# A gated mix of attention and MLP on one core: scores in two 2-bank and three shared 1-bank buffers, a planner that knows the port of VectorE and GpSimd, small scalings on VectorE, two chunks of x transposed by TensorE, another last round

## The chip, the cores and the metric

The kernel runs on one core of one Trainium2 chip. The metric is the device time of one execution in microseconds. Three runs of the kernel before took 892.84, 894.24 and 896.3 us; the median is 894.24 us. Engine names in the rows: PE is TensorE (PEld its weight loads), DVE is VectorE, ACT is ScalarE, POOL is GpSimd, SP is SyncE, which here only issues DMAs.

## The reference

All inputs are bf16; S = 2048 tokens, D = 512, 32 heads of 16, F = 1792.

```python
x = A_x
g = _sigmoid((x * gate_w).sum(-1, keepdims=True))
# A: attention
q, k, v = split_heads(x @ wqkv)                 # 32 heads of 16
p = _softmax(einsum("bhqd,bhkd->bhqk", q, k) * (16 ** -0.5), axis=-1)
a = merge_heads(einsum("bhqk,bhkd->bhqd", p, v)) @ wo
# B: MLP
h = _gelu(_layernorm(x) @ w1)
hs = concat([four 128-column groups of h, shifted by 1, -1, 2, -2 tokens]) @ w2
x1 = x + hs
b = x1 + _gelu(_layernorm(x1) @ w3) @ w4
out = g * a + (1 - g) * b
```

## The kernel before

**Scores.** For each head there are 16 tiles of 128 keys by 512 queries in each of 4 query chunks: 2048 score tiles of 128x512. They are worked off in 32 rounds, one for each chunk c, group G of eight heads and parity p; a round holds 64 tiles, 16 key tiles for each of four heads i that lie in the four 32-row strips of TensorE. A score matmul (L665) writes a tile to PSUM. A tile is exponentiated in one of two ways. ScalarE takes two or three tiles at once from a buffer `psA` of 2 or 3 banks (L741, out `PA`). VectorE takes single tiles from a one-bank `ring` buffer (L766): it turns a score into the bits of a bf16 power of two; two such tiles make a pair of 1024 columns, of which VectorE makes two shifted copies (L790) and GpSimd a third (L793); the four sum to an approximation of exp. A tile of ScalarE thus costs one matmul with V (L821, into `acc`), a tile of VectorE four.

**End of a round.** VectorE copies `acc` to `accsb` (L834, two slots); the row sums go to DRAM and come back 16 to a partition (L837, L839), are inverted and scaled with the gate on VectorE (L841, L842), go out and come back spread over 32 partitions each (L844, L848, `bcs`), GpSimd multiplies (L851, `oT`, two slots), and four DMAs put the result into `oD` (L855, six slots). A slot of `oD` is freed by the output projection of its chunk, which is the tail of the matmul group `w4`.

**Everything else** is a generator ("gen"): groups of column-tiled matmuls (L411) into a ring buffer with one evacuation, mostly on VectorE: the projections of k, q and v, the gate, and w1, w2, w3, w4 of the MLP. The two one-bank ring buffers are shared between gens and VectorE's score tiles. The MLP's layer norms have their statistics and small factors on VectorE and GpSimd, the scaling itself on GpSimd (L529), then go through DRAM and come back by DMA transposes. GpSimd also scales q by two masks (L461), V for the third and fourth copy (L478), and x by 1-g (L587).

**What sets the order.** The order of every engine's instructions is fixed when the kernel is built: a planner (`Sim`) steps through a model of the engines. Each piece of work is a `Job` with an engine, a hold time, dependencies, buffers to take and free, and a priority; `pe_pick` fills TensorE's queue, first scores for free `psA` and ring buffers, then gens and V matmuls until ScalarE is about to be free. A gen may start once as many score tiles have been issued as its `at` says (`spread`, `PLAN`); among the ready ones of the first 24 the one with the smallest `at` goes first. The q of the next group has `at` 128 * r0 - 50, the w4 groups of chunk 0 have 1045 to 1071. On the chip each engine runs its list in order and waits on semaphores.

**Start and end.** Sixteen DMA transposes of x (L364) come first on SP's queue, then x as it stands (L372). The last chunk's output projection (L1053, L1055) follows the last round outside the planner.

## Time and profile before

| what | value |
|---|---|
| median of three runs | 894.24 us |
| the profiled execution | 890.88 us |
| its span, first to last instruction | 888.9 us |
| mean granted TensorE clock | 0.944 |
| ScalarE busy | 755.7 us (85%) |
| TensorE matmul busy (ends modelled) | 786.6 us (89%) |
| VectorE busy | 693.1 us (78%) |
| GpSimd busy | 390.5 us (44%) |

The profiled execution is 3.4 us below the median of the runs, and 2.0 us of it lie outside the span. Busy time of an engine is the union of its instructions; two that follow each other closely overlap by their start-up and drain, so the mean duration of one is longer than what it adds. TensorE's matmuls run four abreast in strips of the array, so its busy share says little about how much more it could take.

### The profile page before, as it was taken

To read this page: it belongs to the slowest core of one execution; us is meant where nothing else is said; L and a number is where in the kernel's file an instruction comes from. 1 tells how busy PE (TensorE), PEld (TensorE's weight loads), DVE (VectorE), ACT (ScalarE), POOL (GpSimd) and SP (SyncE) were. 2 spreads that over 40 slices of the span, in tenths; PEclk is the share of its full clock that TensorE was granted. 3 is DMA by queue.
4 is the path that set the end of the run, shared out by engine and by line. 5 is a ranking of instruction groups with operands and counts; after the bars stand their busy time and mean duration, and the time that the engine had idled before them with its cause. 6 is when DMAs were issued, how large, how long until landed. Compare 5 with 4: busy or idle time off the path is not lost.

```text
span 888.9 us, 22112 instructions
## 1 busy us (share of the span) xinstructions
PE 786.6 (89%) x8981; PEld 251.1 (28%) x8982; DVE 693.1 (78%) x1361; ACT 755.7 (85%) x631; POOL 390.5 (44%) x400
## 2 busy tenths in 40 slices
PE   5996899898898989979898998999988999989982
PEld 1331233322222223322233332333312333323220
DVE  4774988798899998877875787678878568887871
ACT  3364999899998999998993998999998889999990
POOL 2243764444467793434432444234444234344440
PEclk9987999999799999988999996999978999979996
DMA  8512211103013140011000001001000100000001
GB/s 165 168 31 39 82 51 23 38 24 117 17 45 76 46 124 6 18 42 32 14 20 26 24 18 41 26 24 35 18 16 17 30 27 17 14 7 18 18 17 39
DMA packets 71302, 35.83 MB, mean 40 GB/s; under 512 B 51360, under 2 KB 66464, under 8 KB 71200
## 3 DMA queue, kind: packets, MB, share of 16 engines
q1 hardware_dynamic: 68032, 32.84, 14.1%
q10 hardware_dynamic: 3168, 1.57, 0.8%
q8 instruction: 70, 1.15, 0.5%
q14 instruction: 32, 0.26, 0.1%
HBM read 17.60 MB, written 6.82 MB: 27 GB/s over the span
## 4 chain that ended last, share of the span: by engine, by line
PE 48%; ACT 23%; DVE 12%; issue 7%; DMA 4%; POOL 4%; SPq 2%; POOLq 0%; ACTq 0%; DVEq 0%
ACT PA L741 18%; PE acc L821 17%; PE ring L411 17%; PE psA L665 11%; DVE PD L766 5%; DVE PD L790 3%; ACT hT L600 3%; PE ring L665 3%; POOL PD L793 2%; DMA zE_dram<-zE 1%; DVE st L509 1%; POOL xn L529 1%; SPq L364 1%; ACT hT L567 1%; DMA w<-in_A_x_dram 1%
## 5 line engine op out<-in xcount | busy, mean ns | idle before, releaser
L741 ACT ACTIVATE PA<-psA 128x1536 bf16<-128x1536 f32 x614 | 709.7, 1259 | 97.8 <-PE acc L821 38.4
L793 POOL TENSOR_SCALAR PD<-PD 128x1024 uint16<-128x1024 uint16 x257 | 269.8, 1050 | 432.4 <-DVE PD L790 310.4
L766 DVE TENSOR_SCALAR PD<-ring 128x512 uint16<-128x512 f32 x514 | 340.7, 682 | 106.6 <-PE ring L665 90.1
L821 PE MATMUL acc<-PD,V 128*17 128x512 bf16 x2056 | 328.8, 401 | 25.4 <-DVE PD L790 10.5
L821 PE MATMUL acc<-PA,V 128*17 128x512 bf16 x1534 | 292.7, 389 | 2.8 <-DVE accsb L834 2.0
L665 PE MATMUL psA<-q,kT 32*128 32x512 bf16 x1534 | 240.6, 395 | 35.4 <-ACT PA L741 33.5
L790 DVE TENSOR_SCALAR PD<-PD 128x1024 uint16<-128x1024 uint16 x514 | 219.5, 464 | 6.3 <-PE acc L821 0.7
L665 PE MATMUL ring<-q,kT 32*128 32x512 bf16 x514 | 179.1, 402 | 6.1 <-DVE PD L766 5.6
L821 PEld LDWEIGHTS <-V 128*17 128x17 bf16 x3590 | 95.6, 89 | 222.3 <-issue 176.5
L665 PEld LDWEIGHTS <-kT 32*128 32x128 bf16 x2048 | 74.2, 91 | 277.0 <-issue 272.5
L411 PE MATMUL ring<-xnT,w 128*32 128x512 bf16 x1152 | 82.6, 381 | 4.2 <-DVE PD L766 1.3
L411 PE MATMUL ring<-w,hT 128*32 128x512 bf16 x1152 | 84.0, 387 | 1.5 <-DVE x_sb L576 0.8
L411 PEld LDWEIGHTS <-w 128*32 128x32 bf16 x1664 | 45.2, 98 | 56.4 <-issue 32.9
L851 POOL TENSOR_TENSOR oT<-accsb,bcs 128x512 bf16<-128x512 f32 x32 | 41.1, 1283 | 25.1 <-DMA bcs<-rr 18.7
L598 DVE CAST hT<-ring 128x512 bf16<-128x512 f32 x56 | 38.4, 685 | 9.7 <-PE ring L411 9.2
L411 PE MATMUL ring<-w,w 128*32 128x512 bf16 x512 | 44.5, 430 | 1.6 <-DVE PD L766 0.8
L411 PEld LDWEIGHTS <-hT 128*32 128x32 bf16 x1152 | 30.2, 97 | 36.7 <-issue 18.4
L529 POOL TENSOR_SCALAR xn<-x_sb,rs,nm 128x512 bf16<-128x512 bf16 x32 | 29.6, 934 | 1.9 <-DVE nm L522 1.6
L411 PE MATMUL ring<-w,wq 128*32 128x512 bf16 x256 | 20.8, 395 | 8.1 <-DMA w<-in_A_x_dram 6.9
L834 DVE COPY accsb<-acc 128x512 f32<-128x512 f32 x32 | 21.8, 682 | 6.0 <-PE acc L821 5.8
L600 ACT ACTIVATE hT<-hT 128x7168 bf16<-128x7168 bf16 x4 | 24.7, 6177 | 0.0
L509 DVE BATCH_NORM_STATS2 st<-x_sb 128x6 f32<-128x512 bf16 x32 | 21.7, 679 | 0.1
(49 smaller groups left out, 213.4 us busy)
## 6 DMA issues: line engine op xcount, KB each, us to landing
bcs<-rr SPq DMA_DIRECT2D x128, 64.0 KB
xn_dram<-xn SPq DMA_DIRECT2D x32, 128.0 KB
w<-in_B_w_dram SPq DMA_DIRECT2D x5, 512.0 KB
x_sb<-in_A_x_dram SPq DMA_DIRECT2D x4, 512.0 KB
oD<-oT SPq DMA_DIRECT2D x128, 16.0 KB
out_dram<-ot SPq DMA_DIRECT2D x16, 128.0 KB
w<-in_B_w_dram SPq DMA_DIRECT2D x4, 448.0 KB
w<-in_A_wqkv_dram ACTq DMA_DIRECT2D x1, 512.0 KB
```

The source lines that it names most:

```text
L411: units.append([Op("col", j, lambda j=j, lf=lf, rf=rf, st=st, sp=sp: nc.tensor.matmul(get()[32 * j:32 * j + 32, 0:N], lhsT=lf(32 * j, 32 * ...
L509: a = dve(600, deps, lambda: nc.vector.bn_stats(out=sb.slot[:], in_=x_sb[:, t, :]), prio=6, at=at, acq=[sb])
L529: g = gp(760, [m], lambda t=t, xb=xb: nc.gpsimd.tensor_scalar(out=xb.slot[:], in0=x_sb[:, t, :], scalar1=rs[which][:, t:t + 1], scalar2=nm ...
L598: pre.append(evac(g, PSUM_NS, lambda ps, m=m: nc.vector.tensor_copy(out=h2[:, m, :], in_=ps[:]), acq=[bb] if m == 0 else []))
L600: ge = act(93 + 427 * FT + 2600, pre, lambda: nc.scalar.activation(out=h2, in_=h2, func=ACT.Gelu_apprx_tanh), prio=0)
L665: o = Op("row", i, lambda: nc.tensor.matmul(dst(), lhsT=kT[G][32 * i:32 * i + 32, kt * P:(kt + 1) * P], rhs=qbuf[G, c].slot[32 * i:32 * i ...
L741: job = act(hold, ops, lambda: nc.scalar.activation(out=pb.slot[:, 0:n], in_=buf.slot[:, 0:n], func=ACT.Exp, scale=0.25), acq=[pb], frees= ...
L766: nc.vector.tensor_scalar(out=pr["buf"].slot[:, h * 512:(h + 1) * 512], in0=buf.slot[:], scalar1=BITS_MUL, scalar2=BITS_ADD, op0=ALU.mult, ...
L790: nc.vector.tensor_scalar(out=d[k][:, 0:w], in0=d[0][:, 0:w], scalar1=float(SHIFT * k), scalar2=None, op0=ALU.add)
L793: nc.gpsimd.tensor_scalar(out=d[k][:, 0:w], in0=d[2][:, 0:w], scalar1=1.0, scalar2=float(SHIFT), op0=ALU.mult, op1=ALU.add)
L821: o = Op("col", i, lambda: nc.tensor.matmul(acc[32 * i:32 * i + DH + 1, :], lhsT=lhs(), rhs=rhs(), start=st, stop=True, tile_position=(0, ...
L851: n = gp(1250, d3, lambda: nc.gpsimd.tensor_tensor(out=ob.slot[:], in0=ab.slot[:], in1=bb.slot[:], op=ALU.mult), acq=[ob], frees=[ab, bb], ...
```

## The change

- ScalarE's score buffers are two of two banks (before three and two); the ring has three one-bank buffers (before two); `PA` has nine slots (before six).
- The planner marks jobs with `port`: all of GpSimd's, and VectorE's fast SBUF-to-SBUF ones. A marked job isn't started while another holds the port. VectorE's priorities are finer; a pair also takes a token that its GpSimd copy gives back; rounds are kept within 10 to 12 tiles of each other; a DMA holds SP's queue for 450 or 1280 ns in the model (before 60).
- Gens have a due time; the ready one that is due first goes first, and one that is overdue goes ahead of the V matmuls. The q of the next group may start 110 tiles ahead and is due 150 ahead of its first tile.
- The masks of q, the layer norms' scaling, the scaled V and (1-g) x are computed on VectorE.
- Chunks 0 and 1 of x come in as they stand and are transposed by TensorE (32 matmuls of 128x128 against an identity), chunks 2 and 3 by DMA as before. V is projected in two halves of 16 heads, the second between tiles 110 and 253. The exp table is loaded by a dummy activation.
- The last round's row sums are brought to all partitions by matmuls with an identity, the MLP's result of the last chunk is put into PSUM by such a matmul, and the last group's four heads go through their own weight `woL`; no DMA lies between the last score and the output.

In numbers of instructions: exps on ScalarE from 307 of three tiles and 306 of two (and one of one) to 716 of two (and one of one); tiles of VectorE (L766, now L891) 514 to 615; shifted copies on VectorE (L790, now L920) 514 to 614 of 1024 columns and two of 512; copies on GpSimd (L793, now L923) 257 to 307 and one of 512; matmuls 8,982 to 9,679.

```diff
-    WIDTHS, RING = (3, 2), 2
-    NPA, NPD, NW = 6, 16, 9
+    WIDTHS, RING = (2, 2), 3
+    NPA, NPD, NW = 9, 16, 9
...
-            if any(not self.free[b.cls] for b in j.acq):
+            if any(not self.free[b.cls] for b in j.acq) or j.port and self.lock > self.t:
...
+        if j.port:
+            self.lock = self.t + j.hold
...
+    xa, xb = (start(e, 2100.0, lambda q, a=a: q.dma_start(out=x_sb[:, a:a + 2, :], in_=x_src(0, a, a + 2)))
+              for e, a in (("SP", 0), ("ACT", 2)))
...
+    def x_transposes(c, half, dep):
+        g = gen("t", -1, dep + [j_id], [], due=-9 + half)
+        ks = (2 * half, 2 * half + 1)
+        g.units = [[Op("full", None, lambda k=k, t=t: nc.tensor.transpose(
+            out=g.buf.slot[:].bitcast(BF16)[:, (k % 2) * 512 + t * P:(k % 2) * 512 + (t + 1) * P],
+            in_=x_sb[:, 4 * c + t, k * P:(k + 1) * P], identity=idb[:]), ns=54.0, name="t") for t in range(4)]
+            for k in ks]
...
-            j_q[G, c, p] = gp(680, [e, j_m3] + ([j_q[G, c, 0]] if p else []), lambda p=p, m=m: nc.gpsimd.tensor_scalar(
-                out=qb.slot[:, p, :], in0=qf.slot[:], scalar1=m[:], scalar2=1.0, op0=ALU.mult, op1=ALU.mult), prio=0,
+            j_q[G, c, p] = dve(205, [e, j_m3] + ([j_q[G, c, 0]] if p else []), lambda p=p, m=m: nc.vector.tensor_scalar(
+                out=qb.slot[:, p, :], in0=qf.slot[:], scalar1=m[:], scalar2=None, op0=ALU.mult), prio=0.3, port=True,
...
-            g = gp(760, [m], lambda t=t, xb=xb: nc.gpsimd.tensor_scalar(
+            g = dve(205, [m], lambda t=t, xb=xb: nc.vector.tensor_scalar(
...
-            q_proj(G, c, 128 * r0 - 50)
+            q_proj(G, c, 128 * r0 - QAT)
...
-        for g in gens[:24]:
-            if g.at > sim.tiles:
-                break
-            if not sim.free["ring"]:
-                return None
-            if all(d.done is not None for d in g.deps):
-                return g
-        return None
+        if not sim.free["ring"]:
+            return None
+        best = None
+        for g in gens:
+            if g.at <= sim.tiles and (best is None or g.due < best.due) and all(d.done is not None for d in g.deps):
+                best = g
+        return best
...
+        if g is not None and g.due <= sim.tiles:
+            do_gen()
...
+    nc.scalar.copy(out=ab[:, 256:512], in_=acc[:, 256:512])
+    nc.vector.tensor_copy(out=ab[:, 0:256], in_=acc[:, 0:256])
+    for b in range(4):
+        nc.tensor.matmul(pd[:, 4 * b:4 * b + 4], lhsT=ab[:, b * P:(b + 1) * P], rhs=idf[:, 0:P:32], start=True, stop=True)
...
+    nc.vector.reciprocal(out=rdl[:], in_=pd.rearrange("p (b j) -> p b j", j=4))
...
+            nc.tensor.matmul(bc[32 * j:32 * j + 32, b * P:(b + 1) * P], lhsT=rdl[:, b, j:j + 1].to_broadcast([P, 32]),
+                             rhs=idf[:], start=True, stop=True, tile_position=(0, 32 * j), skip_group_check=True)
```

SP's queue at the start of the program, before; `w` are chunks of transposed x, `x_sb` is x as it stands:

```order
L364 DMA_TRANSPOSE w_121<-in_A_x_dram 128x512 x4
L364 DMA_TRANSPOSE w_122<-in_A_x_dram 128x512 x4
L364 DMA_TRANSPOSE w_123<-in_A_x_dram 128x512 x4
L364 DMA_TRANSPOSE w_124<-in_A_x_dram 128x512 x4
L372 DMA x_sb<-in_A_x_dram 128x4x512 x4
```

The same queue now:

```order
L414 DMA x_sb<-in_A_x_dram 128x2x512
L419 DMA x_sb<-in_A_x_dram 128x4x512
L412 DMA w_135<-in_A_wqkv_dram 128x4x256
L423 DMA_TRANSPOSE w_132<-in_A_x_dram 128x512 x4
L412 DMA w_134<-in_A_wqkv_dram 128x4x384
L412 DMA wq<-in_A_wqkv_dram 128x4x384
L423 DMA_TRANSPOSE w_133<-in_A_x_dram 128x512 x4
L412 DMA w_135<-in_A_wqkv_dram 128x4x256
```

The plain loads of x stand first, and eight of the sixteen transposes are left.

VectorE where chunk 0's output rows (`ot`) are made, before; the `accsb` copy here ends round 16, and `qf` is the q of chunk 2's second group:

```order
L766 TENSOR_SCALAR PD_107<-ring_97 128x512
L624 SCALAR_TENSOR_TENSOR ot_152<-ring_98,omg,x_sb 128x512
L766 TENSOR_SCALAR PD_107<-ring_97 128x512
L790 TENSOR_SCALAR PD_115<-PD_107 128x1024
L790 TENSOR_SCALAR PD_111<-PD_107 128x1024
L624 SCALAR_TENSOR_TENSOR ot_153<-ring_98,omg,x_sb 128x512
L598 CAST hT<-ring_98 128x512 x2
L459 CAST qf_138<-ring_98 128x512
L834 COPY accsb_140<-acc 128x512
L598 CAST hT<-ring_98 128x512
L766 TENSOR_SCALAR PD_113<-ring_97 128x512
```

The same place now; the `accsb` copy here ends round 15, one round earlier, and the two q masks stand on VectorE:

```order
L891 TENSOR_SCALAR PD_129<-ring_100 128x512
L748 SCALAR_TENSOR_TENSOR ot_161<-ring_102,omg,x_sb 128x512
L920 TENSOR_SCALAR PD_124<-PD_129 128x1024
L920 TENSOR_SCALAR PD_114<-PD_129 128x1024
L748 SCALAR_TENSOR_TENSOR ot_162<-ring_101,omg,x_sb 128x512
L748 SCALAR_TENSOR_TENSOR ot_161<-ring_100,omg,x_sb 128x512
L970 COPY accsb_150<-acc 128x512
L891 TENSOR_SCALAR PD_119<-ring_102 128x512
L562 CAST qf_147<-ring_100 128x512
L920 TENSOR_SCALAR PD_117<-PD_119 128x1024
L564 TENSOR_SCALAR q_146<-qf_147,mE 128x512
```

Chunk 0's output rows come a round earlier against the ends of the rounds, and six evacuations in a row (`ot`, `hT`, `hT`, `qf`, `accsb`, `hT`) have become three.

VectorE at the end of the program, before:

```order
L790 TENSOR_SCALAR PD_117<-PD_108 128x1024
L834 COPY accsb_141<-acc 128x512
L841 RECIPROCAL pk_159<-pk_159 128x16
L842 TENSOR_TENSOR pk_159<-pk_159,gpk 128x16
L1055 SCALAR_TENSOR_TENSOR ot_152<-ring_97,omg,x_sb 128x512
```

The same end now:

```order
L920 TENSOR_SCALAR PD_121<-PD_120 128x512
L1201 COPY accsb_150<-acc 128x256
L1208 RECIPROCAL rdl<-psA_103 128x16
L1209 TENSOR_TENSOR rdl<-rdl,zE 128x16
L1215 TENSOR_TENSOR oT_154<-accsb_150,psA_103 128x256 x2
L1226 TENSOR_SCALAR ot_161<-ring_100,omg 128x512
```

Before, a DMA stands between `accsb` and the reciprocal and again between the scaled `pk` and the last rows; now each row's input is in PSUM or SBUF.

## Rows read from the trace of the kernel before

**Rows 1.** The page: span, and each engine's busy time, share and instructions.

```profile
span 888.9 us, 22112 instructions
PE 786.6 (89%) x8981; PEld 251.1 (28%) x8982; DVE 693.1 (78%) x1361; ACT 755.7 (85%) x631; POOL 390.5 (44%) x400
```

**Rows 2.** Windows: stretch, length, busy us by engine (instructions), clock, DMA share, GB/s.

```profile
0.00:100.00 100.00, 79.14 (x858) 25.68 (x858) 64.26 (x133) 53.14 (x47) 38.80 (x52) 0.91 0.41 97
100.00:850.00 750.00, 687.85 (x7990) 219.78 (x7989) 613.40 (x1199) 688.10 (x573) 342.93 (x341) 0.96 0.12 33
850.00:889.00 39.00, 19.66 (x140) 5.67 (x135) 15.40 (x31) 14.45 (x14) 8.77 (x8) 0.77 0.11 32
200.00:300.00 100.00, 90.23 (x970) 27.14 (x967) 90.39 (x183) 93.76 (x76) 61.17 (x66) 0.95 0.23 64
...
126.40:156.10 29.70, 28.53 (x333) 9.38 (x331) 25.63 (x52) 29.62 (x26) 12.65 (x14) 1.00 0.15 34
```

**Rows 3.** Lines by form: shapes, count, busy us, mean ns, idle before, releasers.

```profile
L741 ACT ACTIVATE PA<-psA 128x1536 bf16<-128x1536 f32 x307 | 451.8, 1472 | 81.8 <-PE ring L665 31.5 <-PE acc L821 30.1 <-PE psA L665 18.8
L766 DVE TENSOR_SCALAR PD<-ring 128x512 uint16<-128x512 f32 x514 | 340.7, 682 | 106.6 <-PE ring L665 90.1 <-PE psA L665 15.2
...
L741 ACT ACTIVATE PA<-psA 128x1024 bf16<-128x1024 f32 x306 | 320.5, 1047 | 15.9 <-PE acc L821 8.3 <-PE psA L665 5.9 <-PE ring L665 1.4
...
L793 POOL TENSOR_SCALAR PD<-PD 128x1024 uint16<-128x1024 uint16 x257 | 269.8, 1050 | 432.4 <-DVE PD L790 310.4 <-PE ring L665 40.1 <-PE acc L821 34.3
...
L790 DVE TENSOR_SCALAR PD<-PD 128x1024 uint16<-128x1024 uint16 x514 | 219.5, 464 | 6.3 <-PE acc L821 0.7
...
L529 POOL TENSOR_SCALAR xn<-x_sb,rs,nm 128x512 bf16<-128x512 bf16 x32 | 29.6, 934 | 1.9 <-DVE nm L522 1.6
```

**Rows 4.** Timeline of ScalarE, 10 to 100 us: start, length, what, idle before it.

```profile
12.56 2.37 ACT L741 ACTIVATE PA<-psA 128x1536 bf16<-128x1536 f32 x2
...
27.89 2.37 ACT L741 ACTIVATE PA<-psA 128x1536 bf16<-128x1536 f32 x2 [5.88 <-PE acc L821]
...
82.67 2.53 ACT L741 ACTIVATE PA<-psA 128x1536 bf16<-128x1536 f32 x2 [9.52 <-PE psA L665]
```

**Rows 5.** Timeline of VectorE, 64 to 84 us.

```profile
77.86 0.25 DVE L841 RECIPROCAL pk<-pk 128x16 f32<-128x16 f32 x1 [7.95 <-DMA pk<-den]
```

**Rows 6.** Timeline of SP's queue, 0 to 64 us.

```profile
0.72 20.79 SPq L364 DMA_TRANSPOSE w<-in_A_x_dram  x16
```

**Rows 7.** Timeline of all engines, 472 to 492 us.

```profile
480.87 1.04 PE L411 MATMUL ring<-wo,oD 128*32 128x512 bf16 x16
...
483.12 5.07 SPq L855 DMA_DIRECT2D oD<-oT  x8
...
486.38 1.27 POOL L851 TENSOR_TENSOR oT<-accsb,bcs 128x512 bf16<-128x512 f32 x1 [6.43 <-DMA oD<-oT]
...
489.70 3.73 ACT L741 ACTIVATE PA<-psA 128x1536 bf16<-128x1536 f32 x3 [14.58 <-PE acc L821]
```

**Rows 8.** The chain that ended last, from 845 us: start, length, what.

```profile
863.04 1.45 ACT PA L741
...
866.16 1.69 DMA den<-accsb
...
879.84 5.55 PE ring L1053 x13
885.41 0.75 DVE ot L1055
```

**Rows 9.** Timeline of VectorE, 128 to 140 us: two shifts, then two tiles.

```profile
131.83 0.76 DVE L790 TENSOR_SCALAR PD<-PD 128x1024 uint16<-128x1024 uint16 x2
132.51 1.28 DVE L766 TENSOR_SCALAR PD<-ring 128x512 uint16<-128x512 f32 x2
```

**Rows 10.** Timeline of GpSimd and VectorE, 857 to 863 us.

```profile
858.46 1.27 POOL L851 TENSOR_TENSOR oT<-accsb,bcs 128x512 bf16<-128x512 f32 x1
...
858.80 1.55 DVE L790 TENSOR_SCALAR PD<-PD 128x1024 uint16<-128x1024 uint16 x2
```

364 lines of the change are left out of this document (249 added, 115 removed).

## The prediction

> **What bounds the kernel now.** I read the page's busy shares first, then the windows, because the shares average over three different stages, then the lines by form, and at last the timelines of the two ends and of the longest wait of ScalarE. On the page [rows 1] ScalarE is busy 85% of the span, TensorE 89% with modelled ends, VectorE 78%, GpSimd 44%: no engine is full. The windows [rows 2] show why. In the first 100 us ScalarE works 53.14 us, so 46.9 us are lost; from 100 to 850 us it works 688.1 of 750, 61.9 lost; of the last 39 us it works 14.45, 24.5 lost. In the middle ScalarE sets the pace: in a stretch that nothing disturbs (126.4 to 156.1 us) it is busy 29.62 of 29.70 us while VectorE is busy 25.63. So a change pays by what it takes from ScalarE in the middle, as long as another engine does not fill up first, and by what it takes from the two ends.
>
> The ends. ScalarE's first exp starts at 12.56 us, and it waits again and again for V matmuls, since score buffers and PA are full while V is not there: 5.88 us before 27.89, 9.52 us before 82.67 [rows 4]. SP's queue is busy with 16 transposes of x for 20.79 us [rows 6]. At the other end the last exp ends at 863.04 + 1.45 = 864.5 us, and 24.4 us pass to the end of the span: the first DMA hop starts at 866.16 and the last matmuls only at 879.84 [rows 8], so 13.7 us of DMA hops, one small multiplication and waits lie between.
>
> The longest wait: before 489.70 us ScalarE stands for 14.58 us [rows 7]. The rows tell the chain. The output projection of chunk 0 (L411 from oD) runs until 481.9; only then are oD slots free, SP issues eight oD DMAs from 483.12 on, GpSimd's oT, which had waited 6.43 us for them, runs at 486.38, an accsb slot comes free, and the round can end. No score of a later round was allowed to run meanwhile.
>
> **The change part by part.** The sum is made against the profiled execution, 890.9 us, and moved to the runs' median at the end.
>
> *The last round.* What goes: 13.7 us between the first hop and the last matmuls, of which GpSimd's multiplication is 1.3. What stays: V matmuls, a copy of acc (two halves on two engines), output, its DMA; 885.41 + 0.75 = 886.2 to 888.9 is 2.7 us for that DMA. What is new on the path: four small matmuls, a reciprocal and a small product, 20 matmuls that start the fourth bank, 16 that spread the factors, two half-width products, 16 output matmuls, two evacuations one after the other on each of two engines. For matmuls I take the pace of the old last ones with their waits, 13 in 5.55 us, as upper bound of a group of four (0.43 us) [rows 8]: about 14 groups, at most 6 us, and 3 if they run close; full fp32 operands have no row here and may double that. The VectorE steps are 0.68 us at most, as L766 [rows 3], half for half the width: about 3.4 us. So 0.5 + 3.4 + 4 + 2.7 = 10.6 us after the last exp instead of 24.4. I take -13 us, with -10 (matmuls twice as dear) and -15.5 as ends.
>
> *The start.* Eight transposes of 1.30 us (20.79 / 16) leave SP's queue and half of V's projection leaves the first rounds; the first chunk is transposed from a plain load, so the first exp should start at about 10 to 11 us. The waits on V matmuls shrink with V, and nine PA slots stand in place of six. What stays, at least in part, is the 9.52 us wait: VectorE stood for 7.95 us before the reciprocal of round 0's row sums, whose DMA came behind the gate's way through DRAM [rows 5], and the product behind it needs the gate in both programs. Of the 46.9 us I take a third: -16, with -6 (only the earlier exp and half of the queue) and -25 as ends.
>
> *The long wait.* Chunk 0's output rows stand a round earlier against the rounds in VectorE's new list, and the block of six evacuations is three. I take -12 of 14.6, with -4 and -14.6 as ends. If oD slots still come late, the wait is back.
>
> *The middle, ScalarE's side.* A column costs (1472 - 1047) / 512 = 0.83 ns [rows 3]. 1433 tiles in place of 1534 are 51,712 columns less: -42.9 us. But there are 103 instructions more, and each has a fixed part: 1047 - 850 = 197 ns alone, less the overlap of neighbours, which is 0.12 us (a mean of 1.26 against 29.62 / 26 = 1.14 in the undisturbed stretch [rows 2, 3]): 0.077 x 103 = +7.9. Together -35, of which 573 / 614 fall in the middle: -33.
>
> *The middle, VectorE's side.* 101 tiles more at 0.60 us (1.28 us for two, less one drain [rows 9]) are 61 us; 101 shifts more at 0.34 (131.83 to 132.51 holds two) are 34 us. 90 scalings come over from GpSimd: 32 xn, 30 q, 16 V, 12 x. No row shows one on VectorE; a shift of twice their columns takes 0.34, so they lie between 0.17 (half) and 0.34; I take 0.21 as some part is fixed: 19 us, 15 to 31. GpSimd loses these (32 xn alone were 29.6 us at 934 ns) and gains 50 copies of 1.05: 52 us. It stays far from full. VectorE goes from 693 to 807 us if nothing else changes. Two things can give some back. The shifts took 219.5 / 514 = 0.427 us each against 0.38 in an undisturbed pair: 24 us are collisions with GpSimd, and the new list puts two tiles between a pair's shifts and the next shifts, beside which GpSimd's 1.05 us fits. And L766 counts 0.66 us each (340.7 / 514) since many stand alone; close behind each other they take 0.60: 31 us. So 752 to 807 us.
>
> In the middle, VectorE's 613.4 us become 668 to 719, in 735 us of old time (750 less the wait). The best 100 us that I find hold 90.39 [rows 2]. At that share VectorE would need 739 to 795 us, that is +4 to +60; by ScalarE alone the middle would take 735 - 33. I take -8: VectorE at its lower figure and 92% busy, a little above the best seen, because the added work (shifts, tiles) has its input ready earlier with a third ring buffer and the list was made with the port in it. TensorE gets 8% more matmuls (9,679 for 8,982) and two refills for each pair of exps where a smaller buffer drains in 0.93 us in place of 1.35; that is a reason not to take more.
>
> A row on the port: VectorE's two shifts at 858.80 took 1.55 us instead of 0.76; GpSimd's oT ran from 858.46 to 859.73 [rows 10]. The first shift started and got nowhere until GpSimd was done: 0.79 us lost. The Trainium skill, "SBUF — State Buffer", section "Who interferes with whom", says that VectorE in its two-port modes and GpSimd exclude each other for the whole instruction, whichever comes first. The trace agrees with it in this row, and by that rule each of the 90 scalings moved to VectorE adds a place where this can happen.
>
> Sum: 890.9 - 13 - 16 - 12 - 8 = 842, and 845 against the median, which lies 3.4 above the profiled execution.
>
> **The rivals.**
>
> *ScalarE keeps its whole gain.* VectorE and TensorE have room, idle gaps stay as they are: 845 - 25 = 820. For it: 18% of VectorE's middle is idle today. Against: the same gaps must now take over 50 us of work.
>
> *VectorE is the bound.* It stays near 90% with collisions avoided only in part: +4 to +30 in the middle in place of -8, 857 to 883, some 868. For it: nothing busier than 90.39 is seen. Against: in that window gens and layer norms crowd it, too.
>
> *Slower.* The place is the port in the middle: real times slip against the planner's, and the 706 fast VectorE operations meet GpSimd's 354 or so long ones by chance. The price is 0.79 us for each meeting [rows 10]; today it is 24 us, some 30 such meetings. On a full VectorE each lies on the path. From about 68 more than forecast, (899 - 845) / 0.79, the kernel is slower than before: one operation in seven, some 900 us. Against: today it is one in seventeen without any planning.
>
> *It doesn't do what it says.* The long wait stays, since oD still has six slots: 857; this falls into the second rival's stretch.
>
> **How the numbers follow.** The forecast, 832 to 857 us: 0.49. ScalarE alone, 810 to 832: 0.19. VectorE as bound, 857 to 885: 0.25. Port, 899 and more: 0.05. Rest 0.02. The range for 8 in 10 is 818 to 876: it takes in most of the first rival and two thirds of the second. Half a per cent is about what a measurement of this kernel can tell from no change (890 to 899 us): faster 0.93, same 0.03, slower 0.04.
>
> **What the new profile would show.** The last exp's end to the end of the span: about 11 us in place of 24.4. ScalarE's idle time in the first 100 us: about 31 in place of 46.9, with the first exp at 10 to 11. No wait of ScalarE over 5 us between 100 us and the end. L920 at 0.39 or so a piece by busy time in place of 0.427; above 0.5 the port rival holds. The 512-column scalings about 0.2 us in place. VectorE's middle at 92% busy or above; if ScalarE is over 95% busy there, the first rival holds. I am wrong if the middle takes longer for each round than now, or if ScalarE idles over 45 us in the first 100.

## The result and the profile after

The changed kernel takes 860.8 us (median of four runs, 859.9 to 861.8); the kernel before, run beside it, took 893.54. The ratio is 0.9633 (95% interval 0.9602 to 0.9663). The time lies inside the range of 818 to 876 us, but 16 us above the forecast of 845 and just outside its own band of 832 to 857. The profiled execution took 860.45 us, its span 858.7 at a mean granted TensorE clock of 0.962 (before 0.944); how much of the gain is the clock's, no run separates.

The page of the changed kernel, where [rows 1] stood for before:

```profile
span 858.7 us, 24104 instructions
PE 794.5 (93%) x9715; PEld 253.8 (30%) x9715; DVE 785.6 (91%) x1657; ACT 735.1 (86%) x743; POOL 379.6 (44%) x369
```

VectorE has 92 us more work in a span that is 30 us shorter. ScalarE has only 20.6 us less. The windows of the changed kernel (start:end, length, then busy us of TensorE, its weight loads, VectorE, ScalarE and GpSimd with instructions, clock, DMA share, GB/s), the counterpart of [rows 2]:

```profile
0.00:100.00 100.00, 89.00 (x1302) 35.83 (x1302) 83.31 (x196) 74.84 (x82) 35.59 (x45) 0.93 0.40 94
100.00:820.00 720.00, 674.53 (x8077) 206.06 (x8074) 678.34 (x1414) 638.81 (x638) 331.66 (x313) 0.97 0.13 34
820.00:859.00 39.00, 31.01 (x342) 11.96 (x339) 23.91 (x50) 21.44 (x25) 12.39 (x12) 0.94 0.09 24
```

In the middle TensorE is 93.7% busy, VectorE 94.2% and ScalarE 88.7%. Before, ScalarE and TensorE stood there at 91.7% each (688.10 and 687.85 of 750 us) [rows 2]; the prediction named ScalarE alone as what sets the pace. VectorE went past the 90.39% that I had found as its best, and still did not carry ScalarE along.

The same in ScalarE's time, by the two profiled executions (us):

| part | before | after | difference | forecast |
|---|---|---|---|---|
| ScalarE's work | 755.7 | 735.1 | -20.6 | -33 |
| its idle time in the first 100 us | 46.9 | 25.2 | -21.7 | -16 |
| its idle time after the last exp | 23.9 | 14.6 | -9.3 | -13 |
| the longest wait of the middle | 14.6 | 8.7 | -5.9 | -12 |
| its other idle time in the middle | 47.8 | 75.1 | +27.3 | +25 |
| span | 888.9 | 858.7 | -30.2 | -49 |

Before, a last exp of one tile ends at 864.98 us, after the one at 864.49 that the prediction took for the last, so 23.9 us follow it and not 24.4. Now 16.3 follow, of which ScalarE works 1.75. In the column of forecasts the middle's -8 is split into ScalarE's side, -33, and the +25 of idle time that remains. Of the 19 us by which the sum was missed, 12 are ScalarE's own work, 6 the long wait, 4 the last round and 2 the idle time of the middle; the start gave 6 more than forecast.

The ends of the rounds tell the same more plainly. Each is a copy of `acc` (L834 before, L970 and for the last one L1200 now); here are the times at which some of them start (us):

| round | before | after | lead of the changed kernel |
|---|---|---|---|
| 0 | 62.7 | 41.4 | 21.3 |
| 14 | 424.1 | 410.7 | 13.4 |
| 15 | 446.6 | 441.9 | 4.7 |
| 16 | 488.2 | 465.6 | 22.6 |
| 31 | 865.4 | 844.0 | 21.4 |
| end of the span | 888.9 | 858.7 | 30.2 |

The whole lead at the last round was there at the end of the first. Up to round 15 the changed kernel loses some 16 us of it, the long wait of the kernel before gives that back in round 16, and the 15 rounds after that take as long as before. So the middle, long wait and all, gave nothing, where -20 was forecast; the gain is 21 us at the start and 9 after the last round.

The lines of the changed kernel by form (line, engine, out<-in, shapes, count | busy us, mean ns | idle before and what ended it), the counterpart of [rows 3]:

```profile
L866 ACT ACTIVATE PA<-psA 128x1024 bf16<-128x1024 f32 x716 | 683.9, 1029 | 100.5 <-PE ring L789 51.6 <-PE psA L789 38.7 <-remote 5.6
L891 DVE TENSOR_SCALAR PD<-ring 128x512 uint16<-128x512 f32 x615 | 400.9, 679 | 26.9 <-PE ring L789 18.9 <-remote 5.6 <-POOL PD L923 0.7
...
L920 DVE TENSOR_SCALAR PD<-PD 128x1024 uint16<-128x1024 uint16 x614 | 260.1, 464 | 1.8
...
L636 DVE TENSOR_SCALAR xn<-x_sb,rs,nm 128x512 bf16<-128x512 bf16 x32 | 11.3, 405 | 0.0
...
L564 DVE TENSOR_SCALAR q<-qf,mE 128x512 bf16<-128x512 bf16 x15 | 5.4, 357 | 0.0
...
L694 DVE TENSOR_SCALAR x_sb<-x_sb,omg 128x512 bf16<-128x512 bf16 x12 | 4.2, 414 | 0.0
...
L978 DVE TENSOR_TENSOR pk<-pk,gpk 128x16 f32<-128x16 f32 x31 | 5.0, 162 | 2.9 <-DMA gpk<-zE_dram 2.9
...
L629 DVE SCALAR_TENSOR_TENSOR nm<-mv,rs 128x4 f32<-128x4 f32 x8 | 1.1, 142 | 0.0
```

Of ScalarE's 100.5 us of idle time before exps 90.3 are put down to score matmuls (L789), in 119 waits of which the longest is 8.7 us. I read them as the refill of two-bank buffers and, for the ones put down to `ring`, the matmul ahead of it in TensorE's queue. The shifts stayed at 0.424 us each (260.1 / 614; 0.427 before). In the traces 38 of the 614 last over 0.55 us, 40 of 514 before; all 38 start while an operation of GpSimd runs, and what they take beyond the median of 0.42 us comes to 28.9 us (23.6 before). So these collisions were not planned away. The 512-column scalings that came over cost 0.35 to 0.41 us, not 0.21.

ScalarE's timeline in the first 100 us, the counterpart of [rows 4]:

```profile
11.32 0.59 ACT L536 CAST kT<-ring 128x512 bf16<-128x512 f32 x1 [2.57 <-PE ring L495]
12.53 4.70 ACT L866 ACTIVATE PA<-psA 128x1024 bf16<-128x1024 f32 x5 [0.62 <-PE psA L789]
...
63.62 4.97 ACT L866 ACTIVATE PA<-psA 128x1024 bf16<-128x1024 f32 x5 [5.59 <-remote]
```

The first exp is no earlier than before (12.53 for 12.56). The gain of this stretch is that ScalarE waits less on V afterwards: before, 22.1 us in the first 100 were put down to V matmuls (`acc`), now none. A wait of 5.59 us ends at 63.62, put down to "remote", that is, to no event that the profile has. VectorE stands at the same time:

```profile
63.59 0.69 DVE L891 TENSOR_SCALAR PD<-ring 128x512 uint16<-128x512 f32 x1 [5.55 <-remote]
```

SP's queue in these microseconds; L606 writes the gate's 2048 numbers to DRAM, L609 reads them back and waits for that:

```profile
52.13 0.39 SPq L606 DMA_DIRECT2D zE_dram<-zE  x1
53.49 1.15 SPq L646 DMA_TRANSPOSE xnT<-xn_dram  x1
63.68 2.70 SPq L609 DMA_DIRECT2D gpk<-zE_dram  x4
```

The two engines go on within 0.1 us of the issue at 63.68, for which the gate's DMA, which left at 52.13, has to have landed. TensorE stood too, and ran at half its clock afterwards. Its timeline, and the window of 63.6 to 71 us (columns as in the windows above):

```profile
64.69 0.61 PE L789 MATMUL psA<-q,kT 32*128 32x512 bf16 x2 [4.79 <-ACT PA L866]
```

```profile
63.60:71.00 7.40, 5.19 (x52) 1.84 (x51) 4.55 (x10) 4.90 (x5) 1.05 (x1) 0.50 0.28 57
```

The same DMA took 11.3 us in the kernel before (issued at 66.39, read at 77.66), and TensorE stood for 7.0 us there, up to 78.45; the prediction's 9.52 us wait of ScalarE is at this place.

All engines where chunk 0's output rows (`ot`) are made, the counterpart of [rows 7]:

```profile
437.32 0.75 DVE L748 SCALAR_TENSOR_TENSOR ot<-ring,omg,x_sb 128x512 bf16<-128x512 f32 x1 [3.92 <-PE ring L495]
...
441.20 0.75 DVE L748 SCALAR_TENSOR_TENSOR ot<-ring,omg,x_sb 128x512 bf16<-128x512 f32 x1 [3.13 <-PE ring L495]
...
441.87 0.68 DVE L970 COPY accsb<-acc 128x512 f32<-128x512 f32 x1
...
442.02 1.94 ACT L866 ACTIVATE PA<-psA 128x1024 bf16<-128x1024 f32 x2 [8.72 <-PE psA L789]
```

VectorE stands twice for output-projection matmuls, the `accsb` copy that ends round 15 is queued behind, and ScalarE waits 8.72 us. The cause is not the old one: GpSimd's `oT` no longer waits for oD slots (L987 waits for `bcs` alone). TensorE's part is this window:

```profile
432.13:441.53 9.40, 9.40 (x156) 4.27 (x155) 2.35 (x5) 1.17 (x2) 1.62 (x2) 1.00 0.09 30
```

TensorE is busy throughout, by its modelled ends: 144 matmuls of two `w4` groups with their output projection stand in its list in a row, nine V matmuls among them and no score.

All engines at the end of the changed kernel, the counterpart of [rows 8]:

```profile
837.17 5.20 ACT L866 ACTIVATE PA<-psA 128x1024 bf16<-128x1024 f32 x6
...
844.45 0.42 DVE L1201 COPY accsb<-acc 128x256 f32<-128x256 f32 x1 [3.10 <-ACT accsb L1200]
...
847.71 1.42 PE L495 MATMUL ring<-wo,oD 128*32 128x512 bf16 x12
...
849.07 1.05 PE L1203 MATMUL psA<-idf,accsb 128*128 128x4 f32 x8
...
854.07 0.69 ACT L1224 ACTIVATE ot<-ring,omg 128x512 bf16<-128x512 f32 x1 [9.65 <-PE ring L1221]
```

The last exp ends at 842.37, and 16.3 us follow instead of 10.6. The copies of `acc` start at 844.04, 1.2 us later than forecast, and are done at 844.87, but the matmuls that read them (L1203) start at 849.07, behind output-projection matmuls (L495) that were let into TensorE's queue only after the last score.

### The profile page after: what moved, and what is told of

It reads as the page before. It is cut to its first block, busy times and chain, and to the rows that moved or that the text cites. A ratio compares the mean times of both kernels' runs of the same rounds, so it can differ in the third digit from the quotient of the medians.

```text
span 858.7 us, 24104 instructions
## 1 busy us (share of the span) xinstructions
PE 794.5 (93%) x9715; PEld 253.8 (30%) x9715; DVE 785.6 (91%) x1657; ACT 735.1 (86%) x743; POOL 379.6 (44%) x369
## 4 chain that ended last, share of the span: by engine, by line
PE 41%; DVE 36%; ACT 11%; issue 5%; DMA 5%; SPq 1%; ACTq 0%; POOL 0%; DVEq 0%; POOLq 0%
PE acc L954 15%; PE ring L495 14%; DVE PD L891 14%; DVE PD L920 11%; PE psA L789 11%; ACT PA L866 7%; ACT hT L707 2%; DMA pk<-den 2%; DVE st L616 2%; DMA zE_dram<-zE 1%; DVE accsb L970 1%; DVE hT L706 1%; DVE x_sb L685 1%; DVE V L579 1%; DVE xn L636 1%
## 5 line engine op out<-in xcount | busy, mean ns | idle before, releaser
L866 ACT ACTIVATE PA<-psA 128x1024 bf16<-128x1024 f32 x717 | 684.4, 1029 | 100.5 <-PE ring L789 51.6
L923 POOL TENSOR_SCALAR PD<-PD 128x1024 uint16<-128x1024 uint16 x308 | 326.1, 1060 | 446.4 <-DVE PD L920 298.1
L891 DVE TENSOR_SCALAR PD<-ring 128x512 uint16<-128x512 f32 x615 | 400.9, 679 | 26.9 <-PE ring L789 18.9
L954 PE MATMUL acc<-PD,V 128*17 128x512 bf16 x2460 | 339.5, 395 | 21.1 <-DVE PD L920 7.4
L789 PE MATMUL psA<-q,kT 32*128 32x512 bf16 x1433 | 270.7, 392 | 23.8 <-ACT PA L866 22.4
L954 PE MATMUL acc<-PA,V 128*17 128x512 bf16 x1433 | 283.4, 388 | 0.4 <-DVE accsb L970 0.4
L920 DVE TENSOR_SCALAR PD<-PD 128x1024 uint16<-128x1024 uint16 x616 | 260.5, 464 | 1.8
L789 PE MATMUL ring<-q,kT 32*128 32x512 bf16 x615 | 201.7, 398 | 5.9 <-DVE PD L891 5.5
L789 PEld LDWEIGHTS <-kT 32*128 32x128 bf16 x2048 | 72.6, 91 | 286.0 <-issue 284.0
L495 PE MATMUL ring<-xnT,w 128*32 128x512 bf16 x1152 | 84.8, 382 | 1.6 <-DVE PD L891 1.3
L495 PE MATMUL ring<-w,hT 128*32 128x512 bf16 x1152 | 81.3, 388 | 1.1 <-DVE PD L891 0.9
L495 PEld LDWEIGHTS <-w 128*32 128x32 bf16 x1920 | 45.3, 96 | 49.6 <-issue 32.9
L987 POOL TENSOR_TENSOR oT<-accsb,bcs 128x512 bf16<-128x512 f32 x31 | 40.6, 1311 | 9.4 <-DMA bcs<-rr 9.4
L495 PEld LDWEIGHTS <-hT 128*32 128x32 bf16 x1152 | 28.3, 97 | 37.7 <-issue 19.2
L495 PE MATMUL ring<-w,w 128*32 128x256 bf16 (+1 forms) x768 | 36.2, 316 | 0.7 <-DVE PD L891 0.4
L970 DVE COPY accsb<-acc 128x512 f32<-128x512 f32 x31 | 21.1, 679 | 2.7 <-PE acc L954 2.7
L495 PE MATMUL ring<-wo,oD 128*32 128x512 bf16 x240 | 20.9, 380 | 0.0
L495 PE MATMUL ring<-w,wq 128*32 128x512 bf16 x256 | 18.4, 382 | 2.3 <-DVE PD L891 1.4
```

Of the source, the lines that this page charges most:

```text
L495: units.append([Op("col", j, lambda j=j, lf=lf, rf=rf, n0=n0, n1=n1, st=st, sp=sp: nc.tensor.matmul(get()[32 * j:32 * j + 32, n0:n1], lhsT ...
L789: o = Op("row", i, lambda: nc.tensor.matmul(dst(), lhsT=kT[G][32 * i:32 * i + 32, kt * P:(kt + 1) * P], rhs=qbuf[G, c].slot[32 * i:32 * i ...
L866: job = act(hold, ops, lambda: nc.scalar.activation(out=pb.slot[:, 0:n], in_=buf.slot[:, 0:n], func=ACT.Exp, scale=0.25), acq=[pb], frees= ...
L891: nc.vector.tensor_scalar(out=pr["buf"].slot[:, h * 512:(h + 1) * 512], in0=buf.slot[:], scalar1=BITS_MUL, scalar2=BITS_ADD, op0=ALU.mult, ...
L920: nc.vector.tensor_scalar(out=d[k][:, 0:w], in0=d[0][:, 0:w], scalar1=float(SHIFT * k), scalar2=None, op0=ALU.add)
L923: nc.gpsimd.tensor_scalar(out=d[k][:, 0:w], in0=d[0 if both else 2][:, 0:w], scalar1=1.0, scalar2=float(SHIFT * (k if both else 1)), op0=A ...
```

## The experiments

Each was run beside the kernel before on the same chip; the ratio is to that. The changed kernel's own ratio is 0.9633 (0.9602 to 0.9663), 860.8 us. A ratio's interval reaches 3 to 5 us to either side, so differences of a few us are not settled. All but the first two were planned anew, so each has another order of everything.

**Is VectorE the bound? Less of its shifts.** From pair 20 on:

```diff
+                    w_ = w if k == 1 or num < 20 else 256
-                    nc.vector.tensor_scalar(out=d[k][:, 0:w], in0=d[0][:, 0:w], ...
+                    nc.vector.tensor_scalar(out=d[k][:, 0:w_], in0=d[0][:, 0:w_], ...
```

> The changed kernel with the same order, in which from the 21st pair on VectorE's second shifted copy covers 256 of its 1024 columns only; the rest of that buffer keeps older bits, so part of the attention is not computed. VectorE loses some 287 x 0.20 = 57 us of work, no other engine loses any. Theory (VectorE is what bounds the middle): 30 to 50 us faster than the changed kernel, 811 to 831 us. Rival 1 (TensorE's list is the bound): within 8 us of 861. Rival 2 (no engine, the waits between them in a balanced order): 10 to 25 us faster, 836 to 851.

845.5 us, ratio 0.9467 (0.9426 to 0.9508). The shifts in the lines by form of this run:

```profile
L922 DVE TENSOR_SCALAR PD<-PD 128x1024 uint16<-128x1024 uint16 x327 | 140.2, 433 | 1.8
L922 DVE TENSOR_SCALAR PD<-PD 128x256 uint16<-128x256 uint16 x288 | 89.6, 311 | 0.0
```

A shift of a quarter of the columns still takes 0.311 us by this view, so the groups lost 30.3 us (260.1 less 229.8); VectorE's busy time on the page fell by 46.8 (785.6 to 738.8), which I put down to the end of a short shift lying beside the next instruction. The kernel gained 15, as rival 2 had it: a half to a third of what was taken away. VectorE bounds it only in part.

**Is TensorE the bound? Fewer V matmuls.** The fourth copy's matmuls with V are left out from pair 20 on:

```diff
+                leave = k == 3 and num >= 20
...
-        o = Op("col", i, lambda: nc.tensor.matmul(acc[...], lhsT=lhs(), rhs=rhs(), ...
+        o = Op("col", i, None if leave else lambda: nc.tensor.matmul(acc[...], lhsT=lhs(), rhs=rhs(), ...
```

> The changed kernel with the same order, in which from the 21st pair on the V matmuls of the fourth copy (GpSimd's) are left out, so part of the attention is not computed. TensorE loses 574 matmuls, 574 / 4 x 0.22 = 31 us of its list, and no longer waits for GpSimd there; VectorE and ScalarE lose nothing. Theory (VectorE bounds the middle): within 8 us of 861. Rival 1 (TensorE bounds it): 20 to 31 us faster, 830 to 841. Rival 2 (waits in a balanced order): 8 to 18 us faster.

853.56 us, 0.9558 (0.9522 to 0.9594): 7 us, just inside the theory's 8 and by its interval not apart from rival 2; rival 1 with its 20 us fell. But the 31 us are an estimate that this run does not bear out: by the page TensorE's busy time fell by 11.5 us only (794.5 to 783.0). 7 us for 11.5 is a larger part than VectorE's, so TensorE as what bounds the middle is not excluded. The two results together say that work comes back in part at either engine.

**The scalings back on GpSimd.** The four small scalings as before, the rest of the change kept:

```diff
-            g = dve(205, [m], lambda t=t, xb=xb: nc.vector.tensor_scalar(
+            g = gp(760, [m], lambda t=t, xb=xb: nc.gpsimd.tensor_scalar(
```

and the same for q, V and (1-g) x.

> The changed kernel with the 90 small scalings (layer norms' output, q masks, scaled V, (1-g) x) on GpSimd again, planned anew with the port in the model. VectorE loses about 30 us by the new trace (90 merged scalings), GpSimd gains some 65. Theory (VectorE bounds the middle): 8 to 25 us faster, 836 to 853. Rival (the port: GpSimd's long scalings hold up VectorE's shifts, and q comes later): 3 to 15 us slower, 864 to 876, with the busy time of a shift above 0.45 us.

876.8 us, 0.9809 (0.9775 to 0.9844). From the lines by form of this run:

```profile
L920 DVE TENSOR_SCALAR PD<-PD 128x1024 uint16<-128x1024 uint16 x626 | 279.3, 493 | 2.1
```

The rival came, a little beyond its range, with the shift just short of its 0.45. GpSimd's busy time rises to 448.3 us and a shift to 0.446 us (279.3 / 626): 65 shifts last over 0.55 us where 38 did, and what they take beyond the median goes from 28.9 to 45.9 us. So VectorE, with 30 us of scalings taken away, is 6.5 us busier (792.1); 12 more tiles and shifts of the new plan are in that, too. Moving the scalings was worth 16 us, although VectorE pays 0.35 to 0.41 us for each. How much of the 16 is the shifts' and how much comes of q being later was not separated.

**The planner without the port.** The lock is never set, so GpSimd's and VectorE's marked jobs may be planned together:

```diff
-            self.lock = self.t + j.hold
+            self.lock = 0.0
```

> The changed kernel planned without the port: VectorE's fast jobs and GpSimd's are placed as if they never met; all else as it is. Theory (the port in the model keeps VectorE's shifts out of GpSimd's way and VectorE is full): 8 to 25 us slower than the changed kernel, 869 to 886, with the busy time of a shift 0.45 us or more in place of 0.423. Rival (the two tiles between the shifts do it anyway): within 6 us of 861, and the shift as it is.

874.95 us, 0.9793 (0.9744 to 0.9841), as the theory had it in time. But the shifts stay at 0.427 us. The collisions show elsewhere; from the lines by form of this run:

```profile
L978 DVE TENSOR_TENSOR pk<-pk,gpk 128x16 f32<-128x16 f32 x31 | 9.0, 290 | 4.4 <-DMA gpk<-zE_dram 4.3
...
L564 DVE TENSOR_SCALAR q<-qf,mE 128x512 bf16<-128x512 bf16 x15 | 6.7, 447 | 0.0
...
L629 DVE SCALAR_TENSOR_TENSOR nm<-mv,rs 128x4 f32<-128x4 f32 x8 | 5.2, 656 | 0.0
```

The same `nm` of four columns took 142 ns in the changed kernel and takes 656 here, `pk` 162 and 290. The two stood between in the kernel before:

```profile
L842 DVE TENSOR_TENSOR pk<-pk,gpk 128x16 f32<-128x16 f32 x32 | 8.4, 262 | 1.8 <-DMA gpk<-zE_dram 1.5
...
L522 DVE SCALAR_TENSOR_TENSOR nm<-mv,rs 128x4 f32<-128x4 f32 x8 | 3.6, 453 | 0.6 <-POOL rs L520 0.6
```

VectorE is busy 797.6 us, 12 more. The port's cost, 0.79 us in one meeting [rows 10], is real, and the planner avoids it for these small operations; that the shifts would show it was wrong (42 of 618 last over 0.55 us here, 38 of 614 with the lock). That the 12 us are what makes the 14 is likely and not shown, since the order is another one. The Trainium skill, "SBUF — State Buffer", section "Who interferes with whom", which lets a two-port operation of VectorE and GpSimd exclude each other for a whole instruction, agrees with the q rows. The same section says that an operation of VectorE with two SBUF inputs contends with GpSimd's reads; `nm` and `pk`, which have two, bear that out with 0.51 and 0.13 us on average.

**The buffers alone undone.** The whole change but with score buffers of three and two banks, two ring buffers and six PA slots (the last round's fourth and third bank placed to fit):

```diff
-    WIDTHS, RING = (2, 2), 3
-    NPA, NPD, NW = 9, 16, 9
+    WIDTHS, RING = (3, 2), 2
+    NPA, NPD, NW = 6, 16, 9
```

> The changed kernel planned with ScalarE's score buffers of three and two banks, two shared one-bank buffers and six PA slots of 1536 columns, as before the change; the third and fourth bank of the last output come from ScalarE's buffers. ScalarE then has about 51,000 columns more by way of more of its tiles (0.83 ns each, +40 us of work), VectorE some 120 tiles less. Theory (the new buffers move work from ScalarE to VectorE and ease both ways of waiting): 8 to 25 us slower than the changed kernel, 869 to 886. Rival (balanced already, buffers don't matter): within 6 us of 861.

851.97 us, 0.9549 (0.9507 to 0.9591): 9 us faster than with the new buffers, intervals just apart. The theory fell. The page of this run:

```profile
span 850.2 us, 22779 instructions
PE 780.5 (92%) x9337; PEld 260.1 (31%) x9337; DVE 678.0 (80%) x1405; ACT 769.9 (91%) x650; POOL 309.7 (36%) x306
```

And its exps in the lines by form:

```profile
L866 ACT ACTIVATE PA<-psA 128x1536 bf16<-128x1536 f32 x312 | 459.9, 1474 | 32.3 <-PE psA L789 21.5 <-PE ring L789 7.6 <-remote 1.3
...
L866 ACT ACTIVATE PA<-psA 128x1024 bf16<-128x1024 f32 x311 | 325.8, 1048 | 23.6 <-PE psA L789 14.3 <-PE ring L789 7.2 <-PE acc L954 1.6
```

The planner then gives VectorE 489 tiles in place of 615. ScalarE works 34.8 us more but idles 80 us of the span in place of 124, 55.9 of it before exps where it was 100.5. VectorE drops to 80%. The run changes the widths, the ring, the PA slots and with them the split of the tiles at once; which of them gains is not shown by it.

**Gens by start instead of by due time.**

```diff
-            if g.at <= sim.tiles and (best is None or g.due < best.due) and all(...)
+            if g.at <= sim.tiles and best is None and all(...)
...
-        if g is not None and g.due <= sim.tiles:
-            do_gen()
```

> The changed kernel planned without due times: the ready generator with the smallest start goes first, and none goes ahead of the V matmuls because it is overdue; starts as they are. Theory (the order by due time is what shortened the long wait): 5 to 20 us slower, 866 to 881, with a wait of ScalarE above 12 us between 100 us and the end. Rival (the earlier starts alone did it): within 5 us of 861, longest wait below 10 us.

865.83 us, 0.9687 (0.9644 to 0.9731). The interval overlaps the changed kernel's, so this is not settled; if the due times are worth anything, it is some 5 us. The longest wait of ScalarE is 11.7 us here (8.7 with due times), and the one at chunk 0's output rows is 8.9, so the due times are not what made that one short.

**All of x by DMA transposes.** Chunks 0 and 1 as chunks 2 and 3:

```diff
+    for c in (0, 1):
+        for k in range(KT):
+            j_xT[c, 0, k] = start("SP", 1800.0, xT_dma(c, 0, k), 1290.0)
...
-    x_transposes(0, 0, j_x0)
...
-    x_transposes(1, 1, j_x1)
```

> The changed kernel with chunks 0 and 1 of x transposed by DMA too, first on SP's queue after the first plain loads; no transposes by TensorE. Theory (the start's gain is the earlier x): ScalarE's first exp 3 to 6 us later and its idle time in the first 100 us from 25 to 32 or more, 866 to 875 us. Rival (the gain is V in halves and more PA slots, x arrives early enough): within 3 us of 861 and idle time below 29 us.

866.83 us, 0.9706 (0.9664 to 0.9748), 6 us slower, as the theory had it in time (intervals just apart); the first exp moved less than its 3 to 6 us. ScalarE's timeline of this run:

```profile
13.49 0.59 ACT L539 CAST kT<-ring 128x512 bf16<-128x512 f32 x1 [9.60 <-PE ring L498]
14.56 1.94 ACT L869 ACTIVATE PA<-psA 128x1024 bf16<-128x1024 f32 x2 [0.48 <-PE psA L792]
```

The first exp comes 2.0 us later, and ScalarE's idle time in the first 100 us is 32.9 in place of 25.2. So TensorE's transposes are worth 6 to 8 us, although the first exp did not beat the kernel before.

**The gate's row by a matmul.** To test whether the DMA of single numbers holds the engines at 58 to 63.6 us: the gate is turned with the identity on TensorE and leaves as 16 rows of 512 bytes.

```diff
-        d1 = dma(2200.0, [a], lambda: nc.sync.dma_start(out=zE_dram[:].rearrange("(t p) -> p t", p=P), in_=zE[:]))
+        gt.units = [[Op("full", None, lambda: nc.tensor.matmul(gt.buf.slot[0:NT, 0:P], lhsT=zE[:], rhs=idf[:], ...
+        et = sim.add(Job("DVE", 250, 150.0, gt.ops, lambda: nc.vector.tensor_copy(out=zT[:], in_=gt.buf.slot[0:NT, 0:P]),
+        d1 = dma(2200.0, [et], lambda: nc.sync.dma_start(out=zE_dram[:].rearrange("(t p) -> t p", p=P), in_=zT[:]))
```

> The changed kernel in which the gate's exponentials (128 x 16 numbers) are turned to 16 rows of 128 by one matmul with the identity before they go to DRAM, so that this DMA has 16 rows of 512 bytes in place of 2048 single numbers. Theory (the wait of all engines from 58 to 63.6 us is this DMA's): the wait of 5.6 us is gone, 3 to 9 us faster than the changed kernel, 852 to 858. Rival (the wait has another cause, the DMA only ran beside it): the wait stays, within 2 us of 861.

850.8 us, 0.9529 (0.9488 to 0.9571): 10 us faster. SP's queue in this run:

```profile
55.32 0.33 SPq L613 DMA_DIRECT2D zE_dram<-zero  x1
...
59.48 3.09 SPq L616 DMA_DIRECT2D gpk<-zE_dram  x4
```

The row lies in a tile named `zero`. The way out now takes at most 4.2 us (55.32 to 59.48) in place of 11.6, no wait of the "remote" kind is left, and ScalarE works 81.33 us of the first 100. TensorE keeps its full clock where it had 0.50:

```profile
0.00:100.00 100.00, 93.15 (x1403) 37.32 (x1405) 91.49 (x213) 81.33 (x88) 38.23 (x47) 0.97 0.39 97
63.60:71.00 7.40, 6.93 (x91) 2.15 (x83) 7.40 (x17) 7.21 (x8) 3.31 (x4) 1.00 0.09 23
```

Without that DMA the wait is gone, so the rival fell. Of the 10 us, 6.5 are ScalarE's idle time in the first 100 us (18.7 for 25.2), the wait and the slow stretch behind it; the rest comes from other places of a new order. That this DMA alone holds the engines is not shown. It is the same in the run without the port (58.24 to 70.34) and in the one with wide buffers (50.70 to 62.16), and there ScalarE's wait of this kind is none and 1.3 us. What the engines wait for is open: by their modelled ends the scores that they read next were done at 58.2 us.

**Width or crowding? Fewer tiles for VectorE with narrow buffers.** The loss by the buffers could come from the narrow exps or from the work on VectorE that they bring. VectorE's share is capped for each round, buffers as in the change:

```diff
-    DVE_CAP = 119
+    DVE_CAP = 15
```

> The changed kernel, its buffers as they are (two of two banks, three of one), but at most 15 tiles of a round go to VectorE: 479 tiles there in place of 615, and 784 exps of 1024 columns on ScalarE. VectorE loses about 127 us of work, ScalarE gains 68 x 0.95 = 65 us. Theory (the width of ScalarE's buffers is what the three-and-two buffers gained: an exp of two banks leaves TensorE too little time for the refill): slower than the changed kernel by 10 to 40 us, 871 to 901, with ScalarE idle over 110 us. Rival (the split of the tiles is what gained, VectorE was too full): 848 to 858 as with the three-and-two buffers.

910.32 us, 1.0187 (1.0127 to 1.0246). The page and the exps of this run:

```profile
span 909.5 us, 22945 instructions
PE 809.5 (89%) x9307; PEld 249.7 (27%) x9307; DVE 649.0 (71%) x1385; ACT 799.5 (88%) x811; POOL 306.3 (34%) x301
```

```profile
L866 ACT ACTIVATE PA<-psA 128x1024 bf16<-128x1024 f32 x784 | 748.4, 1031 | 85.5 <-PE ring L789 38.6 <-PE psA L789 35.7 <-remote 4.0
```

With 479 tiles on VectorE, close to the 489 of the run with wide buffers, ScalarE has 29.6 us more work and 30 us more idle time than there. 161 more exps (785 for 624) make the work: less 4.3 us for ten tiles, it is (29.6 - 4.3) / 161 = 0.157 us for each added exp. So the width by itself costs ScalarE 25 us of work here. What it costs of the 58 us of time between the two runs isn't clean: the cap puts VectorE's tiles at the start of each round, the granted clock of 100 to 820 us is 0.92 in place of 0.97, and the end is left to ScalarE alone.

**The three small losses together.** With the gate's row by a matmul, chunk 0's output rows planned earlier, and the last groups let in ten tiles before the end:

```diff
-    P_W4 = ((1001, 1054), (1260, 1330), (1560, 1640), (1850, 1940))
+    P_W4 = ((960, 1010), (1260, 1330), (1560, 1640), (1850, 1940))
...
-        return gen("last", TOT, [j_y[tt], dl_w["o"], j_idf] + j_att[NCH - 1][:-1], last_mms(tt), due=TOT)
+        return gen("last", TOT - 10, [j_y[tt], dl_w["o"], j_idf] + j_att[NCH - 1][:-1], last_mms(tt), due=TOT)
```

> The changed kernel with the gate's row by a matmul, the three groups of the last output started 10 score tiles before the end (before: after the last), and w4 of chunk 0 due to start at 960 to 1010 in place of 1001 to 1054. Theory (each is a wait of its own on the path): from 850.8 us 3 to 5 us for the last groups and 3 to 8 us for the long wait at chunk 0's output rows: 838 to 845; the last exp's end to the end of the span 12 to 14 us in place of 16.3, ScalarE's longest wait in the middle below 6 us. Rival (the planner's list is full, what is taken out at one place comes back at the next): 848 to 852.

853.14 us, 0.9559 (0.9514 to 0.9604): nothing beyond the gate's row alone. ScalarE's timeline of this run:

```profile
669.26 1.94 ACT L873 ACTIVATE PA<-psA 128x1024 bf16<-128x1024 f32 x2 [9.92 <-PE psA L796]
```

The same place in the run with the gate's row alone:

```profile
668.06 1.94 ACT L873 ACTIVATE PA<-psA 128x1024 bf16<-128x1024 f32 x2 [10.36 <-PE psA L796]
```

No wait over 2.7 us is left around chunk 0's rows, where the run with the gate's row alone has 7.1 us, but the one at chunk 2's stands as it stood there. In nine of the ten runs that were planned anew it is 8.5 to 12.5 us; the changed kernel with 3.5 us is without it. So what was taken out at chunk 0 did not come back at chunk 2; and yet no time was gained. The last exp ends at 835.48, and 15.0 us follow: the last groups' matmuls still ran behind it, 835.53 to 841. Letting them in sooner did not put them sooner into TensorE's work, and a version that places them before the last scores was not tried.

**The best parts together.** The same with score buffers of three and two banks and two ring buffers:

> All that helped together: score buffers of three and two banks, two ring buffers and six wide PA slots, the gate's row by a matmul, the last output's two groups 10 tiles early, w4 of chunk 0 at 960 to 1010. Theory (the gains stand at different places and add): 852.0 - 9 (gate) - 3 (last) - 4 (long wait) = 836, 828 to 843. Rival (they share one slack): 843 to 850.

847.68 us, 0.9495 (0.9442 to 0.9547), below both kernels. The page of this run:

```profile
span 845.9 us, 22715 instructions
PE 775.8 (92%) x9321; PEld 257.6 (30%) x9321; DVE 672.0 (79%) x1394; ACT 771.7 (91%) x652; POOL 306.1 (36%) x303
```

The buffers gave 9 us alone and the gate's row 10 us alone; both with the rest give 13. The gains are not additive. The rival's reading is that in part they fill the same idle time; no run splits it.

**More slack between rounds.**

```diff
-    SL = (350, 350)
+    SL = (250, 500)
```

on top of the last one.

> As the run before it, and the planner's allowance for how far TensorE's work may run past the point at which ScalarE comes free is 250 and 500 ns by turn, as before the change, in place of 350 for both (a 2-bank exp runs shorter than a 3-bank one). Theory (the allowance fits buffers of unequal width): 2 to 8 us faster than the run before it. Rival (the order changes by chance only): within 3 us of it.

847.59 us, 0.9492 (0.9441 to 0.9543): no difference.

## Why the prediction was right, and where not

*Direction and size from the ends: right.* The start gave 21.7 us (16 forecast), with the fewer waits on V that were named; and with all transposes put back on DMA 6 us are lost. V in halves and the nine PA slots were not tested alone; the run with wide buffers and six slots works no less in the first 100 us (76.96 for 74.84). But "the first exp should start at about 10 to 11 us" was wrong: the transposes, their copies and the k projection end at 12.5, as the DMA way did.

*The last round: -13 forecast, -9.3 measured in ScalarE's idle time, and -7.6 in the time after the last exp (23.9 to 16.3).* The failing step is the list "what is new on the path". I counted the 20 matmuls that start the fourth bank and not the 60 of the other three, which also wait for the last score. They and their queue hold L1203 back from 844.87 to 849.07, 4.2 us.

*The long wait: -12 forecast, -5.9 measured.* "Three evacuations instead of six" was right, and no oD slot comes late, but the two `ot` of the new list still wait 3.92 and 3.13 us for matmuls, with `accsb` behind. Nothing keeps these matmuls: TensorE works through two whole groups, 9.4 us, with no score between. The prediction had VectorE's list for the cause and did not look at TensorE's.

*The middle: the step that failed.* The prediction took -8 us net, "VectorE at its lower figure". Without the long wait ScalarE's middle and its shorter work came out at +6.7 (-20.6 + 27.3). Three terms were mis-sized, and a fourth, TensorE's 8% more matmuls, was named as "a reason not to take more" and put at nothing, though TensorE was as busy as ScalarE.
- The price of an added exp: 0.077 us forecast, 0.157 measured between the two runs with like shares of VectorE. With it, 101 tiles fewer give -42.9 + 0.157 x 103 = -26.7 in place of -35; by the pages the exps fell by 25.3 (709.7 to 684.4). Nine more other instructions on ScalarE (26 for 17) cost 4.7. My 0.12 us of overlap held in a stretch in which exps follow each other without a gap; where exps wait for their buffers, less of it is had, and by all of them: spread over all exps the fixed part is 0.09 us before and in the run with wide buffers, and 0.105 in the changed kernel and in the capped one. (The Trainium skill, "ScalarE: Activation LUTs", section "What ACT_TABLE_LOAD costs", gives 186 ns of fixed part alone and about 93 ns of overlap for neighbours, an estimate of 0.093 net; the kernel before agrees with its 0.09, an added exp at 0.157 does not.)
- The scalings: 19 us taken, 31 as the dear end, and 30 is what they were (11.3 for the 32 xn, 10.6 for the 30 q, 4.2 for x, 3.9 for V).
- "Because the added work has its input ready earlier with a third ring buffer and the list was made with the port in it": the shifts kept 0.424 us each where 0.39 was forecast. The planner's lock is worth 14 us, but not through the shifts: of the old collisions it took away those of `nm` and `pk` (453 to 142 ns and 262 to 162), and left those of the shifts (23.6 us before, 28.9 now).

*The second rival,* VectorE as bound with 857 to 883 us, is where the time fell, and it had a chance of 0.25. Its mechanism holds in part: VectorE is at 94.2% in the middle, and 30 to 47 us less of its work give 15 us. But TensorE, 11.5 us less busy, gives 7, and the wide buffers, which also take 126 tiles from VectorE, give 9. What is shown is three engines at 89 to 94%, and a gain from relieving either VectorE or TensorE. Which of the two bounds more is open.

*The other rivals fell.* ScalarE did not keep its gain (88.7% busy in the middle). The port did not make it slower: shifts at 0.424, not above 0.5. "It doesn't do what it says" is half true, since a wait of 60% of the old length stands at the same rows, for another cause, which is worth 6 us. That the time lies within the range in spite of the middle is in part luck: the start gave 6 us more than forecast.

*What I did not see:* the buffer part of the change is a loss of about 9 us inside a gain of 33, and the gate's DMA, unchanged in the diff, cost 6 to 10.

## What to carry to other kernels

Halving the size of what one engine takes at a time costs its fixed part more often and adds a refill wait each time, and the overlap measured in an undisturbed stretch is not fully had once those waits are there; price both from a stretch that waits. When several engines stand at 90% or more, work taken from one comes back in part only: here a third to a half of VectorE's. Compare the ends of the rounds before and after: they tell at once in which stage a change gained. Work that is let into a queue "at the end" lies on the path of the last result: list all of it, not only what is new there.
